# Where r and late q wait for their stores: pieces of the attention stage moved into the MLP's product buffer

## The chip, the cores and the metric

The kernel runs on one core of one Trainium2 chip. The metric is the device time of one execution in microseconds, the median of several. Before the change it is 825.69 us (median of five, 824.29 to 826.73).

## The reference, cut to what matters

The program computes a transformer block forward and all its gradients. A block is a pre-norm linear attention with a residual, then a pre-norm gated MLP with a residual; S = 2048 rows, D = 640, 32 heads of 20, F = 1728, bfloat16.

```python
phi = lambda t: jnp.where(t > 0, t + 1, jnp.exp(t)) + 1e-6
pq, pk = phi(q), phi(k)
kv  = einsum("bhsd,bhse->bhde", pk, v);  z = einsum("bhsd->bhd", pk)
o   = einsum("bhqd,bhde->bhqe", pq, kv) / (einsum("bhqd,bhd->bhq", pq, z)[..., None] + 1e-6)
h   = x + o_rows @ wo                       # x is layer-normed ahead of wqkv
h2  = h + (silu(hn @ w1) * (hn @ w3)) @ w2  # hn is layer-normed h
# outputs: h2, and the vjp of grad_out to x, wqkv, wo, w1, w3, w2
```

The names below: `pq` is phi(q); `r` is pq with each head divided by its denominator; `M` is the 640 x 640 product of pk and the normed x, from which kv comes; `hh` is the MLP's product silu(gate) * up.

## The kernel before

The rows are cut into 16 tiles of 128. Work is written out by hand in the order in which each engine runs it; no scheduler reorders it. Four instruction streams matter here beside TensorE: VectorE (DVE), ScalarE (ACT), GpSimd (POOL) and SyncE (SP). SP issues loads, stores and all DMA transposes (hardware queue q1); POOL issues stores (software queue q0). A DMA waits on its issuing engine for what it reads, so what is queued behind it on that engine waits too.

**First stage (to about 73 us).** k and q rows are projected and pass through phi; `m_part` and `m_end` build the blocks of M and copy them to `mbs` (4 blocks of 128 x 640); `dz` holds five diagonal 128 x 128 matrices for the denominators. `q_tile` and `q_home` put phi(q): tiles 0 to 3 and 8, 9 into `pq6` (6 tiles), tiles 4 to 7 into four rotating buffers `pql` of pool `pf`, tiles 10 to 13 into spare rows of `pkx`. `r_head`, `r_row` and `r_T` divide a tile in place and transpose it into `pqT` by a DMA transpose on SP.

**Transition (about 73 to 102 us), the tuple of steps in L834 to L842.** TensorE makes the last q tiles (`q_late`, L628) and the combined weight W' (`f2_wT`, L652): block i of W' is copied into `pkx` by ACT and DVE and transposed into `Wp` by a DMA transpose on SP (L660), five blocks, all behind `load_x(0, 4)` (640 KB, L185) on SP. Then `f2_half(t, j)` (L813, matmuls in L618) multiplies pqT by a half of Wp: half j = 0 reads blocks 0 to 2, half j = 1 blocks 2 to 4. The results are added to x, normed (`f2_hn`) and transposed on TensorE (`f2_ht`). In the same tuple POOL issues `r_store(4)`, `r4_out` (r of tiles 0 to 3, 640 KB from pq6, L683), `r_store(5)`, `f2_m_out`, `q_out(8, 10)` (320 KB from pq6, L680), `q_out(10, 14)` (640 KB from pkx) and `r_store(6)`; between the second and the third stands the product `r_prod(7)`, which waits for DVE.

**The MLP (about 102 to 345 us).** Four chunks c of 512 rows, each with 14 column blocks fc. Per block, TensorE makes gate and up (ten matmuls of 512) and one chunk of grad_out @ w2^T (`ghh`), ACT copies them out of PSUM, and per two blocks DVE runs seven products (`mlp_pair`, L768 to L786), of which POOL stores two (`gg_d`, 256 KB each) and SP one (`hh_d`). The four names sig, s2, gate, up rotate over two buffers of pool `pa`, so ACT's copy into `gate` (L749) of pair k waits until the `gg_d<-gate` store of pair k - 2 has landed. PSUM has four `mm` buffers. `hhT[c]`, the chunk's 14 x 512 products per partition (14,336 bytes), rotates over two buffers of `pa`; the next chunk multiplies it by w2. `r_steps` (L875) hangs the remaining q tiles on blocks of the MLP: `r_load(t)` (L689) reads phi(q) of tiles 8 to 15 back from DRAM (`pq_d`) into a `pql` buffer, `r_den` and `r_end` divide and store.

**Memory.** Pools are stacks at the left and right end of the SBUF. On the right lies `pf`, on it `p1` (among others pq6, mbs, dz, pkx), which is released at L843 and whose place `pa` takes; a tile of pa waits for every DMA and engine that still reads what lay there in p1.

**Later stages (345 us to the end)** make the gradients; they are not touched.

Of the kernel before, what the change touches and what calls it, by code (L numbers as in the profile page):

```python
# [9 lines left out]
P = 128  # L10
BF16 = mybir.dt.bfloat16
F32 = mybir.dt.float32
ALU = mybir.AluOpType
# [5 lines left out]
S, D, H, F = 2048, 640, 32, 1728  # L19
DH = D // H  # L20
ST, DT = S // P, D // P
FT, FP = 14, 1792
FL = F - 13 * P
W, SC, TPC = 512, 4, 4
# [31 lines left out]
def kernel(  # L56
# [19 lines left out]
    V, A, T, G, SY = nc.vector, nc.scalar, nc.tensor, nc.gpsimd, nc.sync  # L76
    dma, dmaT, dmaG = SY.dma_start, SY.dma_start_transpose, G.dma_start

    def rows(ap):
        return ap.rearrange("(t p) d -> p t d", p=P)  # L80
# [21 lines left out]
    r_v, pk_v, xn_v, hn_v, m_v, pq_v = rows(r_d), rows(pk_d), rows(xn_d), rows(hn_d), rows(m_d), rows(pq_d)  # L102

    def pool(name, side="left", space=None):
        kw = dict(space=space) if space is not None else dict(side=side)
        return tc.alloc_tile_pool(name=name, bufs=1, reuse_waits="tile", **kw)
# [10 lines left out]
    ident = cp.tile([P, P], BF16, name="ident")  # L117
    make_identity(nc, ident[:])
    ones = cp.tile([P, P], BF16, name="ones")
# [10 lines left out]
    class Stats:  # L130
# [8 lines left out]
        def run(self, src, a, b):  # L139
            for t in range(a, b):  # L140
                for j in range(2):
                    self.part(src, t, j)
# [30 lines left out]


    pf = pool("pf", "right")
    p1 = pool("p1", "right")
    ps = pool("p1p", space=PSUM)
    wqkv = U1.tile([P, DT, 3 * D], BF16, name="wqkv", tag="D")
# [56 lines left out]
    Z = cp.tile([P, DT], F32, name="Z")  # L235
# [14 lines left out]
    def p1_tr(t, parts=((0, DT),)):  # L250
        xn = x_sb[:, t, :]
        for a, b in parts:
            tr = ps.tile([P, DT, P], BF16, name="tr", bufs=2)
            for c in range(a, b):
                T.transpose(tr[:, c, :], xn[:, c * P:(c + 1) * P], ident[:])

            A.copy(out=pqT[:, a:b, t * P:(t + 1) * P], in_=tr[:, a:b, :])  # L257
# [13 lines left out]
    def p1_mm(t, n0, between=None):  # L271
        acc = p1_acc()
        for j in range(2):
            p1_half(acc[:, j, 0:HD], t, n0 + j * HD)
            if j == 0 and between is not None:
                between()
        return acc
# [20 lines left out]
            held.pop(0)()  # L298

    pqs = {}  # L300
    pq6 = p1.tile([P, 6, D], BF16, name="pq")

    def q_home(t):
        if t < 4 or 8 <= t < 10:
# [6 lines left out]
    pkx = []  # L311
# [5 lines left out]
    dz = {}  # L317

    def z_diag(m):
        dz[m] = p1.tile([P, P], BF16, name="dz", bufs=DT)  # L320
        V.tensor_scalar(out=dz[m][:], in0=ident[:], scalar1=Z[:, m:m + 1], scalar2=None, op0=ALU.mult)

    def z_late(ms, acc):

# [8 lines left out]
    def z_rows(parts, acc):  # L333

        for k, ms in enumerate(parts):
            for i, m in enumerate(ms):
                T.matmul(acc[:, k, i * P:(i + 1) * P], lhsT=ones[:], rhs=dz[m][:], start=(i == 0), stop=True,
                         skip_group_check=True)
        for k, ms in enumerate(parts):
            A.copy(out=Zb[:, ms[0] * P:(ms[-1] + 1) * P], in_=acc[:, k, 0:len(ms) * P])  # L340
# [60 lines left out]


    macc = {}
    mbs = p1.tile([P, 4, D], BF16, name="mbs")

    def m_part(m, tiles, js=(0, 1)):
        if m not in macc:
# [102 lines left out]
    for t in range(ST):  # L510
        k = p1_mm(t, D, (lambda: p1_tr(t + 1)) if t + 1 < XT_DMA else None)
# [96 lines left out]
    hn, hnT, hhT = {}, {}, {}  # L608
# [43 lines left out]
    def f2_wT(i):  # L652

        acc = [ps.tile([P, 512], F32, name="wt", tag=("o2", "at")[i % 2], bufs=2) for _ in range(2)]
        for c, a, b, bank, off, first in SQ:
            T.matmul(acc[bank][:, off:off + (b - a) * DH], lhsT=wo[:, c, i * P:(i + 1) * P],
                     rhs=bd[:, c, a * DH:b * DH], start=first, stop=True, skip_group_check=True)
        for bank, (a, b) in enumerate(((0, SPLIT_D), (SPLIT_D, H))):
            (A.copy, V.tensor_copy)[bank](out=pkx[0][:, i, a * DH:b * DH], in_=acc[bank][:, 0:(b - a) * DH])
        dmaT(out=Wp[:, :, i * P:(i + 1) * P], in_=pkx[0][:, i, :])  # L660
# [15 lines left out]
        dmaG(out=pq_v[:, 14:16, :], in_=qx[0][:, 0:4:2, :])  # L676

    def q_out(a, b):
        src = pq6[:, 4:6, :] if a == 8 else pkx[0][:, DT + a - 10:DT + b - 10, :]
        dmaG(out=pq_v[:, a:b, :], in_=src)  # L680

    def r4_out():
        dmaG(out=r_v[:, 0:4, :], in_=pq6[:, 0:4, :])  # L683

    def r_store(a, b):
        for t in range(a, b):
            dmaG(out=r_v[:, t, :], in_=pqs.pop(t))

    def r_load(t):  # L689
        pqs[t] = pf.tile([P, D], BF16, name="pql", bufs=4)[:]  # L690
        dma(out=pqs[t], in_=pq_v[:, t, :])

    def f2_hn(t):
        hn[t] = (pf.tile([P, D], BF16, name="hn", tag="pql", bufs=4) if t == 2 else
# [69 lines left out]
    def drain(n):  # L764
        for _ in range(min(n, len(later))):
            later.pop(0)()
# [63 lines left out]
    def kv3():  # L830
        for m in (2, 3, 4):
            f2_kv(m)

    run((q_late, 10, f2_mT), (q_late, 11, kv3), (phi_rest,), (r_store, 4, 5), (r4_out,),  # L834
        (q_late, 12, lambda: (f2_wT(0), f2_wT(1))), (q_late, 13, lambda: (f2_wT(2), f2_wT(3))),
        (phi_rest,), (q_late, 14, lambda: f2_wT(4)), (load_x, 4, 6), (r_head, 5), (r_prod, 7), (r_store, 5, 6),
        (f2_m_out,), (q_out, 8, 10), (q_out, 10, 14), (load_w2T, 8 * P, 10 * P), (mlp_ghh, 4), (q_late, 15), (sig_table,),
        (f2_half, 0, 0), (f2_half, 1, 0), (f2_half, 2, 0), (f2_half, 0, 1), (f2_half, 1, 1), (f2_hn, 0),
        (f2_half, 2, 1), (f2_hn, 1), (f2_half, 3, 0), (f2_hn, 2), (f2_half, 3, 1), (f2_ht, 0), (mlp_ghh, 5),
        (load_w2T, 10 * P, F), (f2_ht, 1), (mlp_ghh, 6), (r_red, 6, (0,)), (f2_hn, 3), (r_red, 6, (1,)), (f2_ht, 2),  # L840
# [3 lines left out]
    pa = pool("pa", "right")  # L844
# [26 lines left out]
    def r_end(t):  # L871
        r_scale(t)
        r_out(t)

    r_steps = [{2: ((r_load, 8),), 3: ((load_x, 6, 8),), 4: ((r_load, 9),), 5: ((r_store, 7, 8),),  # L875
                10: ((xn_out, 2, dmaG),), 12: ((r_load, 10),)},
               {0: ((r_den, 8), (load_x, 8, 12)), 1: ((r_end, 8), (r_load, 11), (xn_out, 3, dmaG)), 2: ((r_den, 9),), 3: ((r_end, 9), (r_load, 12)),
                4: ((r_den, 10), (q_rest,)), 5: ((r_end, 10), (r_load, 13)), 6: ((r_den, 11),),
# [1 line left out]
               {0: ((r_den, 13),), 1: ((r_end, 13),), 3: ((r_den, 14),), 4: ((r_end, 14),), 6: ((r_den, 15),),  # L880
                7: ((r_end, 15),), 10: ((w_out,),)}, {}]
    for c in range(SC):
        hhT[c] = pa.tile([P, FT, W], BF16, name="hhT", bufs=2)
        o2 = o2_steps(c - 1) if c > 0 else None

        def run_side(pos, fc):
            if c + 1 < SC:
                for f, i in sorted(sides[c][pos].get(fc, ()), key=lambda x: (x[0] is f2_ht, x[1])):
                    f((c + 1) * TPC + i)

        for fc in range(FT):
            mlp(c, fc, lambda: run_side(0, fc))
            drain(1)
            if o2 and not (c == SC - 1 and fc == 5):
                next(o2, None)
            run_side(1, fc)
            drain(1)
            if (c, fc) == (1, 5):
                load_x(12, 16)
            if c == 0 and fc in (5, 7, 9, 11):  # L900
                a, b = {5: (0, 3), 7: (3, 6), 9: (6, 10), 11: (10, 13)}[fc]
                dma(out=w2[:, a:b, :], in_=B_w2[a * P:b * P, :].rearrange("(c p) n -> p c n", p=P))
                if fc == 11:
                    dma(out=w2[0:FL, FT - 1, :], in_=B_w2[(FT - 1) * P:F, :])
            for f, *t in r_steps[c].get(fc, ()):
                f(*t)
            if c == 2 and fc == 3:
                dmaG(out=rows(kvT_d), in_=bd[:])
            if fc == (6, 3, 3)[min(c, 2)] and c < SC - 1:
                load_g2T(c + 1)  # L910
            if c == SC - 1 and fc == 0:
                g2 = U1.tile([P, ST, D], BF16, name="g2", tag="Q")
                tail = U2.tile([P, DT, P], BF16, name="w13tail", tag="g2T", bufs=2)
            if c == SC - 1 and fc in (1, 2, 5, 6):
                i = (1, 2, 5, 6).index(fc)
                dma(out=g2[:, i * TPC:(i + 1) * TPC, :], in_=goS[:, i * TPC:(i + 1) * TPC, :])
            if c == SC - 1 and fc == 8:
                dma(out=tail[:, :, 0:FL], in_=B_w1[:, F - FL:F].rearrange("(c p) f -> p c f", p=P))
                dma(out=tail[:, :, FL:P], in_=B_w3[:, 0:P - FL].rearrange("(c p) f -> p c f", p=P))
            if c == SC - 1 and fc == 9:  # L920
                wT2 = U1.tile([P, DT, D], BF16, name="wT2", tag="MW")
                dmaT(out=wT2[:], in_=w_d[:, :])
# [14 lines left out]
    for _ in o2_steps(SC - 1, A.dma_start, "at"):  # L937
        drain(1)
    pa.release()
    pf.release()  # L940
    ps.release()

# [38 lines left out]
    for fc in range(FT - 1):  # L981
        b, i = divmod(fc, 4)
        if fc == FT - 2:
            gw2_tail()
        acc = ps.tile([P, 2, 512], F32, name="gw", bufs=4)
        for j in range(2):
            for t in range(ST):
                T.matmul(acc[:, j, 0:HD], lhsT=hb[b][:, t, i * P:(i + 1) * P], rhs=g2[:, t, j * HD:(j + 1) * HD],  # L988
                         start=(t == 0), stop=(t == ST - 1))
# [155 lines left out]
    for t in range(ST):  # L1145
# [14 lines left out]
        if t >= 1:  # L1160
# [3 lines left out]
            if t <= 2 * DT:  # L1164
                n = (t - 1) % DT
                dst, src = (woT, A_wo) if t <= DT else (kvN, kvT_d)
# [23 lines left out]
    a, b = ST - 1, ST - 2  # L1190
# [90 lines left out]
    for m, (a, b) in enumerate(M_H):  # L1281
        n = (b - a) * DH
        acc = ps.tile([P, 512], F32, name="gkvT", tag="dkv", bufs=3)
        for c in range(DT):
            T.matmul(acc[:, 0:n], lhsT=woT[:, c, m * P:(m + 1) * P], rhs=QT[:, c, a * DH:b * DH], start=(c == 0),
                     stop=(c == DT - 1))
# [38 lines left out]
    acc = d_acc()  # L1325
    for m in range(DT):
        T.matmul(acc[:, m // 4, m % 4 * P:(m % 4 + 1) * P], lhsT=ones[:], rhs=gzd[:, m, :], start=(m % 4 == 0),
                 stop=True, skip_group_check=True)
# [3 lines left out]
    for t in range(ST):  # L1332
        c, i = divmod(t, TPC)
        u = t // 2
        acc = d_acc()
        for j in range(2):
            for k in range(DT):
                T.matmul(acc[:, j, 0:HD], lhsT=xnT[c][:, k, i * P:(i + 1) * P], rhs=gm[:, k, j * HD:(j + 1) * HD],  # L1338
                         start=(k == 0), stop=(k == DT - 1))
# [7 lines left out]
        if t in (2, 5, 8, 11, 14):  # L1347
            n = t // 3
            acc = square(mN, gkv_b, n)
            k = (4, 0, 1, 2, 3)[n]  # L1350
# [7 lines left out]
        if t in (6, 8, 10, 12):  # L1358
            n = t // 2 - 3
# [110 lines left out]
```

## Time and profile before

| | |
|---|---|
| median of five runs | 825.69 us |
| the profiled execution's own time | 827.82 us |
| its span in the trace | 826.1 us |
| TensorE clock granted | 1.00 |
| busy: TensorE, DVE, ACT, POOL | 815.9, 452.9, 323.7, 133.1 us |
| bytes by queue: q1 (SP), q0 (POOL), q10 (ACT) | 115.54, 24.81, 16.34 MB |
| HBM read and written | 47.33 and 51.46 MB |

How to read it: an idle time is put down to what ended it ("1.94 <-DMA Wp<-pkx": idle 1.94 us, until a DMA into Wp landed). In a group of merged rows the time is from the first start to the last end. The row of a DMA on SPq or POOLq is the time in which its engine issues it, not that of the transfer; the time to landing is listed apart. The share of a DMA queue is the time of its packets over all 16 DMA engines; it can pass 100% because packets overlap. Matmuls are pipelined: five of 128 x 512 in a row start 1.08 us after the five before them when nothing holds them.

### The profile page before, as it was taken

What the parts mean: (1) busy time and instruction counts of PE and PEld (TensorE: products, weight loads), DVE (VectorE), ACT (ScalarE), POOL (GpSimd) and SP (SyncE); (2) the same over time, 40 slices, a digit from 0 to 9 for tenths busy, and PEclk for the clock granted to TensorE, in tenths of its full rate; (3) what the DMA queues carried; (4) which work ended last, traced back from release to release, by engine and by line L of the source; (5) the groups of instructions that cost most, each with busy time, mean ns of one, the idle gap of its engine ahead of it and who ended that gap; (6) DMA issues with size and microseconds to landing.
All of it is one profiled execution on the core that took longest, in us unless ns stands there. A gap on an engine that the chain in (4) does not pass through costs nothing.

```text
span 826.1 us, 14203 instructions
## 1 busy us (share of the span) xinstructions
PE 815.9 (99%) x5549; PEld 523.0 (63%) x5549; DVE 452.9 (55%) x961; ACT 323.7 (39%) x607; POOL 133.1 (16%) x194
## 2 busy tenths in 40 slices
PE   8999899999999999999999999999999999999998
PEld 6777544555555555777777777777777777555554
DVE  7869788899898666400057777772681545200000
ACT  7856577765655666011121221222212334211111
POOL 2244333233323212100001111110220000000000
PEclk9999999999999999999999999999999999999999
DMA  9999979796575565999777787359984798985771
GB/s 226 263 277 238 232 184 269 239 217 175 136 210 158 152 209 161 228 239 271 222 163 181 188 217 180 85 101 184 274 206 96 163 191 181 210 195 136 167 167 38
DMA packets 320947, 157.59 MB, mean 191 GB/s; under 512 B 238704, under 2 KB 314064, under 8 KB 320880
## 3 DMA queue, kind: packets, MB, share of 16 engines
q1 hardware_dynamic: 278768, 115.54, 61.7%
q0 software_dynamic: 7392, 24.81, 8.8%
q10 hardware_dynamic: 34720, 16.34, 8.7%
q8 instruction: 43, 0.70, 0.4%
q14 instruction: 24, 0.20, 0.1%
HBM read 47.33 MB, written 51.46 MB: 120 GB/s over the span
## 4 chain that ended last, share of the span: by engine, by line
PE 85%; DVE 9%; DMA 3%; ACT 1%; issue 1%; POOL 0%; ACTq 0%; DVEq 0%; POOLq 0%
PE job L1234 19%; PE ghn L1033 14%; PE mm L380 11%; PE gxn L1392 8%; PE gw L988 7%; PE o L799 6%; PE big L265 4%; PE gwo L1118 3%; PE macc L411 3%; PE gr L1090 3%; PE dkv L1338 3%; DMA gg_d<-gate 2%; DVE s L774 2%; DVE gate L774 1%; DVE st L147 1%
## 5 line engine op out<-in xcount | busy, mean ns | idle before, releaser
L1234 PE MATMUL job<-gb,hnN 128*128 128x432 bf16 (+2 forms) x656 | 117.0, 342 | 0.0
L1033 PEld LDWEIGHTS <-ggb 128*128 128x128 bf16 x864 | 84.5, 98 | 32.8
L1234 PEld LDWEIGHTS <-hnN 128*128 128x128 bf16 x656 | 63.6, 98 | 53.4
L380 PE MATMUL mm<-pqT,w 128*128 128x512 bf16 x405 | 93.6, 379 | 0.1
L380 PEld LDWEIGHTS <-w 128*128 128x128 bf16 x540 | 52.5, 98 | 63.1 <-issue 1.1
L1238 ACT CAST obs<-job 128x432 bf16<-128x432 f32 (+3 forms) x61 | 29.3, 481 | 123.0 <-PE job L1234 123.0
L799 PE MATMUL o<-w,hhT 128*128 128x320 bf16 x448 | 67.7, 299 | 0.0
L1033 PE MATMUL ghn<-w13a,ggb 128*128 128x320 bf16 x448 | 63.5, 299 | 0.0
L1033 PE MATMUL ghn<-w13b,ggb 128*128 128x320 bf16 x416 | 61.4, 299 | 0.0
L380 PE MATMUL mm<-g2T,w2T 128*128 128x512 bf16 x240 | 59.6, 379 | 0.0
L799 PEld LDWEIGHTS <-hhT 128*128 128x128 bf16 x448 | 43.8, 98 | 23.8 <-issue 0.2
L988 PE MATMUL gw<-g,hb 128*128 128x320 bf16 x416 | 56.8, 299 | 0.0
L1098 POOL TENSOR_TENSOR sz<-Zb,g_h 128x640 f32<-128x640 bf16 x16 | 20.2, 1261 | 198.8 <-DVE g_h L1096 198.8
L988 PEld LDWEIGHTS <-hb 128*128 128x128 bf16 x416 | 40.6, 98 | 16.0 <-issue 0.3
L1392 PE MATMUL gxn<-wqT,gT 128*128 128x320 bf16 x320 | 48.7, 299 | 0.0
L400 ACT CAST ghh<-mm 128x512 bf16<-128x512 f32 x48 | 28.5, 594 | 39.3 <-PE mm L380 34.5
L738 ACT ACTIVATE sig<-mm 128x512 bf16<-128x512 f32 x56 | 33.9, 605 | 24.1 <-PE mm L380 20.1
L1045 ACT ACTIVATE gs<-ghn 128x640 bf16<-128x640 f32 x16 | 11.3, 704 | 78.7 <-PE ghn L1033 78.7
L265 PE MATMUL big<-wqkv,pqT 128*128 128x320 bf16 x260 | 39.9, 299 | 1.5 <-DMA wqkv<-in_A_wqkv_dram 0.9
L380 PEld LDWEIGHTS <-w2T 128*128 128x128 bf16 x260 | 25.3, 98 | 23.3
L265 PEld LDWEIGHTS <-pqT 128*128 128x128 bf16 x320 | 30.6, 98 | 14.3 <-ACT pqT L257 1.2
L1392 PEld LDWEIGHTS <-gT 128*128 128x128 bf16 x320 | 31.3, 98 | 12.2
(208 smaller groups left out, 1280.7 us busy)
## 6 DMA issues: line engine op xcount, KB each, us to landing
hh_d<-hhT SPq DMA_DIRECT2D x24, 256.0 KB, 2.6
gg_d<-gate POOLq DMA_DIRECT2D x24, 256.0 KB, 4.9
gg_d<-ghh POOLq DMA_DIRECT2D x24, 256.0 KB, 3.6
ggb<-gg_d SPq DMA_DIRECT2D x6, 896.0 KB, 5.3
ggb<-gg_d ACTq DMA_DIRECT2D x6, 832.0 KB, 5.9
out_dram<-obs ACTq DMA_DIRECT2D x39, 108.0 KB, 3.1
x_sb<-in_A_x_dram SPq DMA_DIRECT2D x6, 640.0 KB, 5.9
ggb<-gg_d SPq DMA_DIRECT2D x2, 1728.0 KB, 13.5
```

Source lines behind the costliest of these rows:

```text
L265: T.matmul(acc, lhsT=pqT[:, c, t * P:(t + 1) * P], rhs=wqkv[:, c, n0:n0 + HD], start=(c == 0), stop=(c == DT - 1))
L380: T.matmul(acc[:], lhsT=w[:, c, fc * P:(fc + 1) * P], rhs=rhs[:, c, :], start=(c == 0), stop=(c == DT - 1))
L400: A.copy(out=ghh[n // 2][:, n % 2, :], in_=acc[:])
L411: T.matmul(macc[m][j][:, 0:n], lhsT=pk_all[:, t, m * P:(m + 1) * P], rhs=x_ext[:, t, j * HD:j * HD + n], start=(t == 0), stop=(t == ST - 1))
L738: A.activation(sig[:, i, :], gp[:], AF.Sigmoid)
L774: V.tensor_tensor(out=out, in0=a, in1=b, op=alu)
L799: T.matmul(o2["ps"][:, 0:HD], lhsT=hhT[c][:, fc, i * P:(i + 1) * P], rhs=w2[:, fc, j * HD:(j + 1) * HD], start=(fc == 0), stop=(fc == FT - 1))
L988: T.matmul(acc[:, j, 0:HD], lhsT=hb[b][:, t, i * P:(i + 1) * P], rhs=g2[:, t, j * HD:(j + 1) * HD], start=(t == 0), stop=(t == ST - 1))
L1033: T.matmul(acc[:, j, 0:HD], lhsT=ggb[t // 2][:, k, lo:lo + P], rhs=rhs[:, j * HD:(j + 1) * HD], start=(k == 0), stop=(k == NG - 1))
L1234: T.matmul(acc[:, 0:n], lhsT=lhs[:, t, m * P:(m + 1) * P], rhs=rhs(t), start=(t == 0), stop=(t == ST - 1))
L1238: A.copy(out=ob, in_=acc[:, 0:n])
L1392: T.matmul(acc[:, j, 0:HD], lhsT=g, rhs=wqT[:, k, j * HD:(j + 1) * HD], start=(k == 0), stop=(k == 14))
```

## The change

A new pool `ph` lies between `pf` and `p1`, with one buffer of 14,336 bytes per partition. In the first stage it holds `hx`: the six tiles of pq6, the four blocks of mbs and the five dz matrices (11 x 640 numbers per partition), which leave p1. In the MLP the same buffer is hhT of the chunks 1 and 3; hhT of chunks 0 and 2 has one buffer in `pa`. So the six q tiles stay in place through chunk 0.

Four things follow in the order of the work: `r4_out` goes out of the transition and is issued as two stores of 320 KB, at blocks 1 and 4 of chunk 0; `q_out(8, 10)` is gone, and `r_load(8)` and `r_load(9)` read the tiles from `hx` by a copy inside the SBUF; `r_store(4)` is joined with `r_store(5)`, behind `r_prod(7)` on POOL; pool addresses of p1 and pa shift, and with them the waits of pa's first tiles.

```diff
+    ph = pool("ph", "right")
...
-    pq6 = p1.tile([P, 6, D], BF16, name="pq")
+    hx = ph.tile([P, FT * W], BF16, name="hx", tag="H1")[:, 0:11 * D].rearrange("p (t n) -> p t n", n=D)
+    pq6, mbs = hx[:, 0:6, :], hx[:, 6:10, :]
...
-        dz[m] = p1.tile([P, P], BF16, name="dz", bufs=DT)
+        dz[m] = hx[:, 10, m * P:(m + 1) * P]
...
-    mbs = p1.tile([P, 4, D], BF16, name="mbs")
...
     def q_out(a, b):
-        src = pq6[:, 4:6, :] if a == 8 else pkx[0][:, DT + a - 10:DT + b - 10, :]
-        dmaG(out=pq_v[:, a:b, :], in_=src)
-
-    def r4_out():
-        dmaG(out=r_v[:, 0:4, :], in_=pq6[:, 0:4, :])
+        dmaG(out=pq_v[:, a:b, :], in_=pkx[0][:, DT + a - 10:DT + b - 10, :])
+
+    def r4_out(a, b):
+        dmaG(out=r_v[:, a:b, :], in_=pq6[:, a:b, :])
...
     def r_load(t):
+        src = pqs[t] if t < 10 else pq_v[:, t, :]
         pqs[t] = pf.tile([P, D], BF16, name="pql", bufs=4)[:]
-        dma(out=pqs[t], in_=pq_v[:, t, :])
+        dma(out=pqs[t], in_=src)
...
-    run((q_late, 10, f2_mT), (q_late, 11, kv3), (phi_rest,), (r_store, 4, 5), (r4_out,),
+    run((q_late, 10, f2_mT), (q_late, 11, kv3), (phi_rest,),
         (q_late, 12, lambda: (f2_wT(0), f2_wT(1))), (q_late, 13, lambda: (f2_wT(2), f2_wT(3))),
-        (phi_rest,), (q_late, 14, lambda: f2_wT(4)), (load_x, 4, 6), (r_head, 5), (r_prod, 7), (r_store, 5, 6),
-        (f2_m_out,), (q_out, 8, 10), (q_out, 10, 14), (load_w2T, 8 * P, 10 * P), (mlp_ghh, 4), (q_late, 15), (sig_table,),
+        (phi_rest,), (q_late, 14, lambda: f2_wT(4)), (load_x, 4, 6), (r_head, 5), (r_prod, 7), (r_store, 4, 6),
+        (f2_m_out,), (q_out, 10, 14), (load_w2T, 8 * P, 10 * P), (mlp_ghh, 4), (q_late, 15), (sig_table,),
...
-    r_steps = [{2: ((r_load, 8),), 3: ((load_x, 6, 8),), 4: ((r_load, 9),), 5: ((r_store, 7, 8),),
+    r_steps = [{1: ((r4_out, 0, 2),), 2: ((r_load, 8),), 3: ((load_x, 6, 8),), 4: ((r_load, 9), (r4_out, 2, 4)),
+                5: ((r_store, 7, 8),),
...
-        hhT[c] = pa.tile([P, FT, W], BF16, name="hhT", bufs=2)
+        hhT[c] = (ph.tile([P, FT, W], BF16, name="hhT", tag="H1") if c % 2 else
+                  pa.tile([P, FT, W], BF16, name="hhT"))
...
     pa.release()
+    ph.release()
     pf.release()
```

More of the change, by code (lines that the diff above doesn't have):

```diff
@@ L319, in z_diag @@
     def z_diag(m):
-        dz[m] = p1.tile([P, P], BF16, name="dz", bufs=DT)
-        V.tensor_scalar(out=dz[m][:], in0=ident[:], scalar1=Z[:, m:m + 1], scalar2=None, op0=ALU.mult)
+        dz[m] = hx[:, 10, m * P:(m + 1) * P]
+        V.tensor_scalar(out=dz[m], in0=ident[:], scalar1=Z[:, m:m + 1], scalar2=None, op0=ALU.mult)
     def z_late(ms, acc):
@@ L336, in z_rows @@
             for i, m in enumerate(ms):
-                T.matmul(acc[:, k, i * P:(i + 1) * P], lhsT=ones[:], rhs=dz[m][:], start=(i == 0), stop=True,
+                T.matmul(acc[:, k, i * P:(i + 1) * P], lhsT=ones[:], rhs=dz[m], start=(i == 0), stop=True,
                          skip_group_check=True)
```

## The prediction, made before the result was known

> **What bounds the kernel now.** I read the page first, then TensorE's waits, then the timeline around the longest of them, then the DMA queues in that stretch, and last the MLP's first chunk, where work is put in.
>
> The page, and TensorE's waits (microseconds in total, times, longest):
>
> ```profile
> PE 815.9 (99%) x5549; PEld 523.0 (63%) x5549; DVE 452.9 (55%) x961; ACT 323.7 (39%) x607; POOL 133.1 (16%) x194
> ```
>
> ```profile
> PE at L618 <- DMA Wp<-pkx: 3.7, 2, 1.9
> PE warm L450 <- DVE zero L124: 1.1, 1, 1.1
> ...
> PE at L618 <- DVE rden L359: 0.3, 1, 0.3
> ```
>
> TensorE is idle for 826.1 - 815.9 = 10.2 us of the span. Most of that is the start and the tail; the one wait inside that is worth anything is 3.7 us for the transposes into Wp, in the transition, where the change takes stores away. The timeline of it (start, length, engine):
>
> ```profile
> 76.07 0.60 POOL L687 DMA_DIRECT2D r_d<-pql  x1 [0.98 <-DVE mq L292]
> ...
> 76.67 0.76 POOL L683 DMA_DIRECT2D r_d<-pq  x1
> 76.70 2.94 SPq L370 DMA_TRANSPOSE pqT<-pql  x1
> ...
> 80.62 8.02 SPq L660 DMA_TRANSPOSE Wp<-pkx  x5
> ...
> 87.88 2.20 PE L618 MATMUL at<-Wp,pqT 128*128 128x320 bf16 x15 [1.94 <-DMA Wp<-pkx]
> ...
> 91.94 0.85 PE L618 MATMUL at<-Wp,pqT 128*128 128x320 bf16 x5 [1.73 <-DMA Wp<-pkx]
> ```
>
> TensorE stops at 85.94, waits 1.94 for the third block of Wp, runs three halves, waits 1.73 for the fifth. The reader is to see the second and third row: POOL issues 640 KB of r just as SP issues the transpose ahead of Wp's, and that issue lasts 2.94 us where its like lasts 1.2 (the one at 75.38 lasts 1.22). The DMA queues from 78.9 to 80.5 (packets, MB, share of 16 engines), and the third and fifth transposes into Wp in narrow windows of SP's timeline:
>
> ```profile
> q0 software_dynamic: 143, 0.65, 101.2%
> q1 hardware_dynamic: 16, 0.00, 0.6%
> ```
>
> ```profile
> 83.37 1.99 SPq L660 DMA_TRANSPOSE Wp<-pkx  x1
> ...
> 87.19 1.45 SPq L660 DMA_TRANSPOSE Wp<-pkx  x1
> ```
>
> For 1.6 us the 16 DMA engines move POOL's stores alone; SP's queue stands. It then has to move a transpose, 640 KB of x and the five transposes in turn.
>
> The first chunk of the MLP:
>
> ```profile
> 117.09 0.74 POOL L757 DMA_DIRECT2D gg_d<-gate  x1 [1.68 <-ACT s L739]
> 118.90 0.72 POOL L757 DMA_DIRECT2D gg_d<-ghh  x1 [1.06 <-DVE ghh L774]
> ```
>
> ```profile
> 130.15 2.32 PE L380 MATMUL mm<-pqT,w 128*128 128x512 bf16 x10
> ```
>
> ```profile
> 130.74 0.59 ACT L749 CAST gate<-mm 128x512 bf16<-128x512 f32 x1 [2.46 <-DMA gg_d<-gate]
> ```
>
> ACT's copy into gate waits for a store to land, four times here, 7.1 us between 110 and 147; TensorE does not stand, but barely. The ten matmuls at 130.15 take 2.32 us, their plain time, and the second five (due at 130.15 + 1.08 = 131.23) need the PSUM buffer that this copy frees at 130.74 + 0.59 = 131.33. There is no slack left.
>
> **The change, part by part.** Times are those of the profiled execution: span 826.1, own time 827.82, which is 2.1 over the median of the runs (825.69). I make the sum against 827.82 and carry the difference to the median.
>
> *1. r4_out, and r_store(4), leave the stretch 76 to 81.* That is 640 + 160 KB, the two POOL rows at 76.07 and 76.67. The worth is read from the chain to the fifth block of Wp:
> - First block: its source in pkx is complete when DVE's two casts at 79.67 (0.76) are half through, about 80.1. SP issued it at 80.62, because of the 2.94 us. At 1.2 the issue would be free by 78.0, the load of x (0.71) by 78.8. So the first goes out at about 80.1, 0.5 earlier.
> - Each next one costs 1.2 and a gap of 0.1. The third, then, is issued at 82.7 (was 83.37) and the fifth at 85.3 (was 87.19): the third's 1.99 and a gap of 0.5 before the fifth come from a queue that is behind, and go with it. The sources are there in time (the last DVE cast ends at 83.9).
> - Landing: the fourth took 2.9 us, the fifth 4.7, with POOL's stores of 86.89 to 88.72 beside it. Those start no earlier than now, except r_store(4), and the fifth is now ahead of most of them. I take 3.6: it lands at 88.9, was 91.9.
> - The third, with 3.6 to 4.5, lands at 86.3 to 87.2; three halves of 0.69 end at 88.4 to 89.3. So TensorE takes up the second halves at about 88.9 instead of 91.94: **3.0 us earlier**. No more than 3.67 can come of it. The low end is 0.5, if only the first block's issue moves.
>
> Does it carry on? From 91.94 to 147 TensorE never idles for more than 0.3 us, and DVE's norms (idle until 93.29 for the second halves) follow it; DMAs needed there (x of tiles 4 and 5, issued 88.71, used at 101.58) have over 6 us. So the whole rest moves forward.
>
> *2. r_store(4) behind r_prod(7) on POOL.* It is issued at about 85.9, after r_prod(7) (84.38 + 1.53), and not at 76.07. Nothing on POOL waits longer: the stores behind it waited for DVE until 86.89. Its landing frees the pql buffer that the norm of tile 2 writes at 97.44 (94.4 when 3.0 earlier); the stores' times to landing here are 2.1 to 4.7, so 90.6 at the latest. Cost 0; without that cover it would hold DVE.
>
> *3. q_out(8, 10) goes* (POOL, 0.72 at 88.02, 320 KB). It lay beside the fifth block's landing, counted above. q_out(10, 14) goes out 0.7 earlier for it.
>
> *4. r_load(8) and (9) read the SBUF.* Same two DMAs on SP, 0.44 and 0.53 to issue, at 111.72 and 117.97. The copy within the SBUF has no row; the loads from DRAM landed in 3.7 to 6.9 us, a store from SBUF in 2.1. The tiles are used at 152.01, over 27 us later: 0 at either end.
>
> *5. r4_out in the MLP.* Two POOL issues of about 0.72, 320 KB (0.33 MB) each. On the page q0 moved 24.81 MB in 8.8% of the span, 2.93 us for a MB, so 0.96 us of all DMA engines for each.
> - The first stands behind r_store(6) and a memset (end 105.77) and waits for nothing; POOL's next store is at 111.09, after 5.3 us idle. From 104 to 110 the queues are 7.6% and 15.7% busy: 0.
> - The second stands between the gate store at 117.09 and the ghh store at 118.90; POOL's 1.06 idle there covers its issue. But its data go ahead of ghh, r_store(7) and the third gate store, whose landing (130.7) TensorE has no slack for, and from 117 to 131 the queues are 75.4% and 34.1% busy. Bounds: 0 and, for all 640 KB, 1.92; I take **0.7**, most of one store.
>
> *6. The places.* The tiles of p1 and pa lie elsewhere. In the program, the first sigmoid and the first s product no longer wait for stores of the transition; the last of these, from pkx, landed at 88.72 + 6.3 = 95.0, before 102.80, so 0. The first hhT product of chunk 1 now waits for the second r4_out and r_load(9): about 125 against 148: 0. Matmuls, DVE and ACT work are the same; POOL issues one DMA less.
>
> Sum: 827.82 - 3.0 + 0.7 = 825.5, and from the median 825.69 - 2.3 = **823.4 us**. About 0.2% (1.65 us) is what a measurement of this kernel can tell from no change; 2.3 is 0.28%.
>
> **Two rules beside these rows.** The Trainium skill, "DMA: Bandwidth & Descriptors", section "SWDGE vs HWDGE vs iDMA", says that a DMA engine takes its software and hardware queues in turn. The rows of 78.9 to 80.5 show no such sharing; by the rule the stores would have held SP's queue for half as long, and the sum would lose about 1 us of gain (824.4). The row decides. The same page, "Queues, rings and completion order", speaks against the change: a completion is written only after every earlier write of that DMA engine, on whatever queue. The gate store of 121.81 landed 8.9 us later, close to the transpose of grad_out issued at 120.95 (10.2 us), which fits it. By the rule alone the second r4_out would hold that landing for its whole 0.96, and the sum would be 823.7.
>
> **The rivals.**
> - *No gain: SP's transposes are late by themselves.* Idle DMA engines are seen at 77.5 to 78.4, before any of POOL's bytes move, while SP is in its 2.94; one elsewhere is long without POOL's stores (2.11 at 53.68). Then only the 0.5 of the first issue goes, 0.5 - 0.7 = +0.2: 825.9. Against it: the 0.6% row, and the transpose at 229.34, 2.89 long just after POOL issued 256 and 800 KB.
> - *Slower: r4_out holds the gate stores.* Place: ACT's L749 in chunk 0. If the second gate store (5.3 us to landing, 117.09 to 122.36) lands as late as the third (8.9), TensorE, with 0.2 slack there (copy free at 122.95, needed at 123.12), stands 3.4, and a further 0.96 at the third: 4.4 - 3.0 = +1.4, 827.1. It decides as soon as the stalls there exceed 3.0 us. For it: four waits without slack. Against it: the first half falls into idle queues, and the second is behind that gate store, not ahead.
> - *Full gain: both waits for Wp go and the MLP hides all*: 825.69 - 3.7 = 822.0.
>
> **How the numbers follow.** Forecast (net -1.7 to -3.0) 0.50, full gain (beyond -3.0) 0.13, no gain 0.21, slower rival 0.16. Faster by over 0.2%: 0.13 + 0.47 + 0.02 from the others = 0.62. The slower rival's middle is within 0.2%, but its stalls may recur at later pairs: 0.12 slower, 0.04 within; same 0.03 + 0.19 + 0.04 = 0.26. The range goes from full gain, 821.9, over no gain, to 826.2, leaving about 0.05 below and 0.14 above. The forecast's own range is 822.7 to 824.0.
>
> **What the profile after would show.** The issue of r4's transpose near 1.2 us; Wp's five transposes within 6.5 us from 80.1; TensorE's wait for Wp at 0.7 and not 3.7; the MLP's first matmuls near 98.4 (101.52 now). Chunk 0's gate copies waiting 2 to 3.4 us, with one stall of TensorE under 1. I am wrong if the wait for Wp stays above 2, or if TensorE stands for over 2 us between 110 and 150.

## The result, and the profile after

| | median, us | executions (lowest to highest) |
|---|---|---|
| before | 825.30 | 79 (823.74 to 832.38) |
| after | 824.35 | 44 (823.64 to 826.37) |
| profiled execution, before | 827.82 (span 826.1) | |
| profiled execution, after | 825.21 (span 823.5) | |

The ratio is 0.9984, with a 95% interval of 0.9978 to 0.9991. The kernel is faster by 1.0 us by the medians and by 1.3 us by the ratio, where 2.3 us were forecast. That is about half of the forecast gain. It is inside the stated range (821.9 to 826.2) but outside the forecast's own 822.7 to 824.0, and the 0.16% of the ratio are less than the 0.2% that the prediction thought would more likely than not be passed. Two things in the table matter for what follows. The fastest executions of the two kernels are alike (823.74 and 823.64). And the execution that was profiled before lies 2.5 us above the median of the 79.

TensorE's wait for Wp after (total, times, longest), and the timeline of the transition (start, length, engine):

```profile
PE at L619 <- DMA Wp<-pkx: 1.3, 1, 1.3
```

```profile
77.03 2.20 SPq L372 DMA_TRANSPOSE pqT<-pql  x1
...
79.32 0.53 SPq L186 DMA_DIRECT2D x_sb<-in_A_x_dram  x1
...
81.22 7.04 SPq L661 DMA_TRANSPOSE Wp<-pkx  x5
...
86.83 2.20 PE L619 MATMUL at<-Wp,pqT 128*128 128x320 bf16 x15
86.91 0.60 POOL L687 DMA_DIRECT2D r_d<-pql  x1
...
90.51 0.85 PE L619 MATMUL at<-Wp,pqT 128*128 128x320 bf16 x5 [1.34 <-DMA Wp<-pkx]
```

The wait for the third block is gone and that for the fifth is 1.34 instead of 1.73, so 3.7 us have become 1.3. The transpose of r of tile 4 still takes 2.20 us to issue although no store of POOL is beside it. The row at 86.91 is r_store(4) in its new place.

The first chunk of the MLP: TensorE's matmuls, and ACT's waits for the gate stores between 90 and 150 us.

```profile
100.08 8.80 PE L382 MATMUL mm<-pqT,w 128*128 128x512 bf16 x40
```

```profile
ACT gate L750 <- DMA gg_d<-gate: 3.3, 3, 2.4
```

These waits were 7.1 us and are 3.3, with 640 KB of r added between them. TensorE has no wait here.

To see where time goes, I matched each group of matmuls in the trace of before with the same group in the other trace and took the difference of their starts. For after it is +1.06 us at 70 us (before the transition), -1.43 at 110 us, -2.15 at 230 us, and -2.62 at the end. So the start of this execution lost 1.06; the transition gained 2.49; the MLP gained 0.72 and the tail 0.46. The loss at the start is TensorE waiting for its first loads; it was 0.30 and 0.38 in two further profiles of the same kernel, and 1.21 in one of the kernel before, so it comes and goes.

### The profile page after: what moved, and what is told of

Its sections match the earlier page's. It is cut to its first block, busy times and chain, and to the rows that moved or that the text cites. A ratio compares the mean times of both kernels' runs of the same rounds, so it can differ in the third digit from the quotient of the medians.

```text
span 823.5 us, 14204 instructions
## 1 busy us (share of the span) xinstructions
PE 816.3 (99%) x5549; PEld 523.6 (64%) x5549; DVE 453.3 (55%) x961; ACT 324.5 (39%) x607; POOL 132.6 (16%) x194
## 4 chain that ended last, share of the span: by engine, by line
PE 97%; DMA 1%; SPq 1%; ACT 0%; issue 0%
PE mm L382 20%; PE job L1238 19%; PE ghn L1037 14%; PE gxn L1396 8%; PE o L800 7%; PE gw L992 7%; PE big L266 4%; PE gwo L1122 3%; PE macc L412 3%; PE gr L1094 3%; PE dkv L1342 3%; PE at L619 2%; PE mm L266 1%; DMA g2T<-in_grad_out_dram 1%; PE dkv L1270 1%; PE gp L382 1%
```

## The experiments

Three accounts of the missing half had to be told apart. One: r4_out holds SP's queue in the transition, as forecast, but the profiled execution of before had an unusually long wait for Wp, so that its 3.7 us were not there to be gained in the median. Two: the gain in the transition is the same in every execution, and the MLP takes half of it back through the moved stores of r. Three: the gain has another source (the q tiles that stay in the chip, the new places in memory), and r4_out is not what makes Wp late.

### The two kernels again

> The kernel before, profiled once more: it tells which differences between the two profiles are the kernel's. Theory (the 1.06 us by which the changed kernel's profile is late from the start, 9 to 18 us, is chance): start-up differs from the first profile by up to 1 us, the two waits for Wp are 3.7 +- 0.5 us again. Rival (the new places make the start slower): start-up agrees with the first profile within 0.2 us.

> The changed kernel once more, with times. Theory: 0.997 to 0.999 of before; wait for Wp 1.3 us, once; start-up anywhere between the first profile of before and 1.06 us later; no stall of TensorE in chunk 0 of the MLP. Rival (new places slow the start): start-up late by 1.06 us again. Rival (the second r4_out costs in most executions): TensorE stands 0.5 to 1 us between 115 and 135.

> The kernel before once more, for another profile of its own. Theory (the profiled execution of 827.82 had an extraordinary share of its excess in the wait for Wp): this execution, whatever its time T, waits about 2.2 + (T - 825.5) / 2 us for Wp, so 2 to 3 us when T lies between 825 and 827, and the stalls of 0.2 to 0.3 at about 145 and 195 us are there. Rival (the wait is the same in every execution and the excess lay elsewhere): 3.5 to 3.9 us whatever T is.

> The kernel after once more, beside the two that follow. 824.2 to 824.7; the wait for Wp 1.0 to 1.7 us in one piece; the five transposes within 6.9 to 7.1 us, with the gap of some 0.4 before the fifth.

The kernel after took 824.51 us (825.44 for before on that chip; ratio 0.9988, 0.9980 to 0.9997) and 824.45 us (825.41; 0.9981, 0.9967 to 0.9995). The table has the profile of each of these executions, and of three kernels that follow. "Third" is SP's time to issue Wp's third transpose; "five" is the whole row of five; "fifth lands" is from the issue of the fifth to its landing.

| profile | its own time | r of tile 4: issue | third | five | fifth lands | wait for Wp |
|---|---|---|---|---|---|---|
| before | 827.82 | 2.94 | 1.99 | 8.02 | 4.7 | 3.7 |
| before, second | 826.64 | 2.85 | 1.54 | 7.34 | 3.7 | 2.7 |
| before, third | 826.29 | 2.14 | 1.82 | 7.52 | 3.4 | 1.7 |
| r4_early | 826.08 | 2.89 | 2.09 | 7.81 | 4.2 | 2.8 |
| after | 825.21 | 2.20 | 1.20 | 7.04 | 3.6 | 1.3 |
| after, second | 824.78 | 2.19 | 1.20 | 6.88 | 3.9 | 1.7 |
| after, third | 824.46 | 1.63 | 1.21 | 6.88 | 3.2 | 1.0 |
| before_rT4 | 824.09 | behind | 1.22 | 6.50 | 2.6 | 0 |
| rT4_again | 823.58 | behind | 1.22 | 6.50 | 3.3 | 0.7 |

The waits of the third execution of before, for the row that the verdict rests on:

```profile
PE at L618 <- DMA Wp<-pkx: 1.7, 2, 1.2
```

The wait for Wp in the kernel before is 3.7, 2.7 and 1.7 us in three executions; in the kernel after it is 1.3, 1.7 and 1.0. The forecast rested on the longest one, and the second account falls with it. (The 3.7 us expected of the second execution of before and the 2.6 us expected of the third were too many.) That execution also lacks two short stalls of TensorE, 0.23 us at 145 us and 0.49 us at 195 us, which were expected in it, which the first profile of before has, and which the first profile of after has not. So those 0.72 us in the MLP come and go, and the kernel before can be without them. Whether the change makes them rarer is not shown: a loss of 0.4 to 0.5 us at 195 us is in three of the four profiles with the old memory layout (before three times, and before_rT4, below), and in one of the ten with the new (rT4_late; both_late has some 0.2 us of it).

### r4_out back in the transition

```diff
-    run((q_late, 10, f2_mT), (q_late, 11, kv3), (phi_rest,),
+    run((q_late, 10, f2_mT), (q_late, 11, kv3), (phi_rest,), (r4_out, 0, 4),
...
-    r_steps = [{1: ((r4_out, 0, 2),), 2: ((r_load, 8),), 3: ((load_x, 6, 8),), 4: ((r_load, 9), (r4_out, 2, 4)),
+    r_steps = [{2: ((r_load, 8),), 3: ((load_x, 6, 8),), 4: ((r_load, 9),),
```

> The changed kernel with the store of r of tiles 0 to 3 (640 KB, one DMA) put back to its old place in the transition; q tiles 8 and 9 still stay in the SBUF, r_store(4) stays late. Theory (this store holds SP's transposes): the transition is slower again by 2 to 2.5 us, two waits for Wp of 3 to 3.7 us, time 1.000 of before or up to 1.001. Rival (the places or the 320 KB of q tiles make the gain): the wait for Wp stays 1.3 us and the time stays at 0.998.

Measured: 825.18 us against 824.51 for the kernel after on that chip; the ratio to before is 0.9993 (0.9982 to 1.0003). The waits and the transition of this kernel:

```profile
PE at L619 <- DMA Wp<-pkx: 2.8, 2, 1.5
```

```profile
75.01 0.81 POOL L683 DMA_DIRECT2D r_d<-hx  x1
...
76.01 2.89 SPq L372 DMA_TRANSPOSE pqT<-pql  x1
...
78.99 0.54 SPq L186 DMA_DIRECT2D x_sb<-in_A_x_dram  x1
...
80.13 7.81 SPq L661 DMA_TRANSPOSE Wp<-pkx  x5
```

With r4_out alone put back (r_store(4) stays late), both waits for Wp return (2.8 us, short of the 3 to 3.7 expected), and so do the third's 2.09 us and the row of 7.81. So r4_out does make Wp late in this order of SP's queue. (It goes out at 75.01, earlier than in the kernel before, since r_store(4) is no longer ahead of it.) How much of it the median holds is another matter: this profiled execution took 826.08 us, 0.9 over the median of its kernel and the longest but one, which took 4076.28. By the medians r4_out costs 0.67 us, and part of that is not the wait: the tail, after the last matmuls, is 0.38 us longer than in the kernel after. So some 0.3 us are left for the wait.

### Both stores of r into the block that has no slack

```diff
-    r_steps = [{1: ((r4_out, 0, 2),), 2: ((r_load, 8),), 3: ((load_x, 6, 8),), 4: ((r_load, 9), (r4_out, 2, 4)),
+    r_steps = [{2: ((r_load, 8),), 3: ((load_x, 6, 8),), 4: ((r_load, 9), (r4_out, 0, 2), (r4_out, 2, 4)),
```

> The changed kernel with both halves of r4_out at block 4 of chunk 0, so 640 KB and not 320 go in between the second gate store and the ghh store. It doubles the suspected cost in the MLP. If the 0.7 us of the prediction were there: TensorE stands 1.5 to 2 us in chunk 0, time 0.999 to 1.001. If the store is hidden as the first profile shows: not over 0.3 us slower than the changed kernel, 0.998.

Measured: 824.44 us against 824.51, ratio to before 0.9990 (0.9981 to 0.9999). ACT's waits for the gate stores in this kernel:

```profile
ACT gate L750 <- DMA gg_d<-gate: 2.9, 3, 1.9
```

Doubling the bytes at block 4 neither costs time that these runs can tell nor lengthens the waits. The MLP takes nothing back, and the rival that it does falls.

### Phi(q) of tiles 8 and 9 through DRAM again

```diff
-        dmaG(out=pq_v[:, a:b, :], in_=pkx[0][:, DT + a - 10:DT + b - 10, :])
+        src = pq6[:, 4:6, :] if a == 8 else pkx[0][:, DT + a - 10:DT + b - 10, :]
+        dmaG(out=pq_v[:, a:b, :], in_=src)
...
-        src = pqs[t] if t < 10 else pq_v[:, t, :]
+        src = pq_v[:, t, :]
...
-        (f2_m_out,), (q_out, 10, 14), (load_w2T, 8 * P, 10 * P), (mlp_ghh, 4), (q_late, 15), (sig_table,),
+        (f2_m_out,), (q_out, 8, 10), (q_out, 10, 14), (load_w2T, 8 * P, 10 * P), (mlp_ghh, 4), (q_late, 15), (sig_table,),
```

> The kernel after, but phi(q) of tiles 8 and 9 goes to DRAM in the transition as before (320 KB from POOL, between the store of M and the store of tiles 10 to 13) and is loaded back from there. Theory (the gain is r4_out's and the layout's; those 320 KB are issued after the fifth Wp transpose): the wait for Wp grows by at most 0.5 us over the 1.0 to 1.7 of the kernel after, time 824.4 to 824.9; no stall over 0.1 at about 145 and 195 us. Rival (tiles 8 and 9 staying in the chip are what removes these two stalls): 0.5 to 0.6 us come back there, time 824.9 to 825.4.

Measured: 824.40 us (825.37 for before on that chip; ratio 0.9986, 0.9975 to 0.9997), wait for Wp 1.0 us, and neither of the two short stalls. The kernel after took 824.51 and 824.45 us on the two other chips, and 824.35 in the table at the top. This part of the change is worth nothing that these runs can tell.

### r of tile 4 transposed behind Wp

After the experiments above, 1.0 to 1.7 us of wait are left in the kernel after. Its five transposes begin when the casts let them, but the row is 6.9 to 7.0 us long, since about 0.5 us passes before the fifth, and the fifth takes 3.2 to 3.9 us to land where the three before it take 2.6 to 2.8. Two moves ask what holds it.

```diff
-    r_head(4)
+    r_row(4)
...
-        (phi_rest,), (q_late, 14, lambda: f2_wT(4)), (load_x, 4, 6), (r_head, 5), (r_prod, 7), (r_store, 4, 6),
+        (phi_rest,), (q_late, 14, lambda: f2_wT(4)), (r_T, 4), (load_x, 4, 6), (r_head, 5), (r_prod, 7), (r_store, 4, 6),
```

> The kernel after, but the transpose of r of tile 4 (SP, 2.20 us to issue, the last but one ahead of Wp's first) goes behind Wp's five. Theory (Wp's first is held by the casts into pkx, and the five then follow at 1.3 us each): the first is issued at the same time as in the kernel after, Wp waits 1.0 to 1.7 us, time 824.2 to 824.7. Rival (SP's queue is still behind from that transpose and the load of x): Wp's transposes are issued in 1.2 each without the gap before the fifth, the wait falls under 0.6 us, time 823.2 to 823.8.

> The kernel after with the transpose of r of tile 4 behind Wp's five, once more. If its 823.64 is its own: 0.5 to 1.0 under the kernel after on this chip, 823.4 to 823.9, the five transposes within 6.5 us. If it was the chip's or chance: within 0.3 of the kernel after.

Measured: 823.64 us beside 824.40 for q8_early and 825.37 for before on the same chip (ratio 0.9975, 0.9963 to 0.9987); and 823.59 beside 824.45 for the kernel after and 825.41 for before on another (0.9979, 0.9962 to 0.9997). The five transposes take 6.50 us in both and the wait for Wp is 0.6 and 0.7 us. The first goes out no earlier, as the theory said, but the gap ahead of the fifth is gone and the time falls, as the rival said. The edit is worth 0.8 to 0.9 us on top of the change (on the first chip q8_early stands in for the kernel after).

The traces say more about that gap. SP's rows around it, in after and then in rT4_again:

```profile
85.17 1.20 SPq L661 DMA_TRANSPOSE Wp<-pkx  x1
...
86.88 1.37 SPq L661 DMA_TRANSPOSE Wp<-pkx  x1
```

```profile
86.79 1.32 SPq L372 DMA_TRANSPOSE pqT<-pql  x1
88.56 0.45 SPq L186 DMA_DIRECT2D x_sb<-in_A_x_dram  x1
```

The pause has not gone. It stands two DMAs later, behind all five transposes of Wp, where it costs TensorE nothing. Count the instructions of SP that a trace records (its DMAs and its waits for semaphores): in all 14 profiles a pause of 0.43 to 0.45 us stands ahead of the 80th. That is Wp's fifth transpose where r of tile 4 is ahead of Wp, and the load of x where it is behind. Ahead of the 208th, 336th and 464th, 128 apart each time, SP pauses too, for 0.34 to 0.38 us wherever it does not wait for something else there. So this pause goes with the place in SP's program and not with what its queue holds, and part of what the edit gains is that Wp's fifth transpose comes ahead of that place. Why SP pauses there is not shown by any run.

The second move takes POOL's stores of M and of phi(q) of tiles 10 to 13 away from the fifth block's landing, alone (q10_late) and with the first move (both_late).

```diff
-        (f2_m_out,), (q_out, 10, 14), (load_w2T, 8 * P, 10 * P), (mlp_ghh, 4), (q_late, 15), (sig_table,),
+        (load_w2T, 8 * P, 10 * P), (mlp_ghh, 4), (q_late, 15), (sig_table,),
...
-        (r_inv, 6), (r_scale, 6), (r_T, 6), (mlp_ghh, 7), (f2_ht, 3), (f2_half, 4, 0), (f2_half, 4, 1), (r_red, 7), (r_inv, 7),
+        (r_inv, 6), (r_scale, 6), (r_T, 6), (mlp_ghh, 7), (f2_ht, 3), (f2_half, 4, 0), (f2_half, 4, 1), (f2_m_out,), (q_out, 10, 14), (r_red, 7), (r_inv, 7),
```

> As rT4_late, and the stores of M and of phi(q) of tiles 10 to 13 (640 KB from POOL, issued at 87.4 to 89.8 in the kernel after, beside the landing of the fifth Wp block) go behind, to just before the last reduction of the transition. Theory (the fifth block's landing of 3.6 us is its own, and TensorE's 1.0 to 1.7 us come from the casts and five transposes in a row): time as rT4_late within 0.3. Rival (these stores stretch that landing): it falls from 3.6 to about 2.9 as the fourth's, the wait by 0.7, time 0.7 under rT4_late.

> The kernel after with the stores of M and of phi(q) of tiles 10 to 13 (POOL, 640 KB and M's last block) behind, just before the transition's last reduction; r of tile 4 is transposed where the kernel after does it. If this place of the stores is what cost the kernel with both moves 0.8 over the one with the transpose alone: 0.5 to 1.0 over the kernel after, 824.9 to 825.4, with a new or longer wait in the first blocks of the MLP or at 95 to 105 us. If these stores stretched the fifth block's landing: 0.3 to 0.7 under it. If neither: within 0.3.

Measured: both_late 824.43 us (825.37; 0.9987, 0.9975 to 0.9999), q10_late 824.75 us (825.41; 0.9984, 0.9969 to 0.9999). The fifth block lands in 3.3 us in both and the wait is 0.7 and 1.1 us, so these stores were not what stretched that landing. Nor does the time agree with either expectation of both_late. The later place costs 0.8 us with the first move, by the medians, and 0.3 us alone, which is within the spread of the executions (824.10 to 825.10, beside 823.92 to 825.21 for the kernel after). Both profiles show one thing that the other twelve do not: DVE's first product into hhT, which lies where pkx lay, waits 0.7 us for the moved store of phi(q) (at 106.17 in q10_late), and at 117 us TensorE loses 0.17 (q10_late) and 0.24 us (both_late). That the one leads to the other was not tried, and the rest of the 0.8 us stays open.

### The same transpose, in the kernel before

If the order on SP is what matters, the layout and the moved stores are not needed. This kernel is the one before, with all its stores of the transition where they were, and only the transpose of r of tile 4 behind Wp's:

```diff
-    r_head(4)
+    r_row(4)
...
-            dmaG(out=r_v[:, t, :], in_=pqs.pop(t))
+            dmaG(out=r_v[:, t, :], in_=pqs[t])
...
-        (phi_rest,), (q_late, 14, lambda: f2_wT(4)), (load_x, 4, 6), (r_head, 5), (r_prod, 7), (r_store, 5, 6),
+        (phi_rest,), (q_late, 14, lambda: f2_wT(4)), (r_T, 4), (load_x, 4, 6), (r_head, 5), (r_prod, 7), (r_store, 5, 6),
```

> The kernel before with one thing moved: the transpose of r of tile 4 on SP goes behind Wp's five, while r_store(4), r4_out and both pieces of phi(q) stay in the transition. Theory A (the 640 KB of r4_out hold whatever SP has in its queue then, now the load of x and Wp's first transposes): the wait for Wp stays at 1.7 to 3.7 us, time 825.0 to 825.8, and the executions keep their spread (825.4 plus or minus 1.2). Theory B (the long issue of that one transpose, 2.1 to 2.9 us, is what the stores stretch, and Wp's are late only as they are queued behind it): the first of Wp goes out at 80.15 and the five take 6.5 us, wait 0.6 to 0.9, time 823.7 to 824.3.

Measured: 823.82 us (823.26 to 824.64) beside 825.41 for before and 824.45 for after on the same chip. That is 1.6 us under before by the medians; the ratio, 0.9964 (0.9945 to 0.9982), says 3.0 us, as it counts the long executions of before on that chip (up to 832.19). All that TensorE waits for in this kernel, and its transition:

```profile
PE warm L450 <- DVE zero L124: 1.1, 1, 1.1
PE big L265 <- ACT pqT L257: 0.4, 1, 0.4
PE big L265 <- DMA wqkv<-in_A_wqkv_dram: 0.3, 1, 0.3
PE at L618 <- DVE rden L359: 0.3, 1, 0.3
```

```profile
76.16 0.60 POOL L687 DMA_DIRECT2D r_d<-pql  x1 [0.98 <-DVE mq L292]
...
76.53 1.49 SPq L185 DMA_DIRECT2D x_sb<-in_A_x_dram  x1
...
76.76 0.76 POOL L683 DMA_DIRECT2D r_d<-pq  x1
...
80.25 6.50 SPq L660 DMA_TRANSPOSE Wp<-pkx  x5
...
88.20 0.85 PE L618 MATMUL at<-Wp,pqT 128*128 128x320 bf16 x5
```

There is no wait for Wp at all. The 800 KB of r go out at 76.16 and 76.76 as before, and the queues show them just as dense; from 78.98 to 80.58 (packets, MB, share of 16 engines):

```profile
q0 software_dynamic: 112, 0.55, 96.0%
q1 hardware_dynamic: 4, 0.01, 0.9%
```

So the stores still stop SP's queue for 1.6 us, but that no longer matters with one transpose less in it ahead of Wp's. Theory A falls; theory B holds in the time and in the 6.50 us of the five, while its 0.6 to 0.9 us of wait were too many. With the transpose of r of tile 4 ahead of Wp's, the wait is 1.0 to 1.7 us without r4_out on POOL (the kernel after) and 2.8 with it (r4_early). With the transpose behind, it is 0.6 and 0.7 us without r4_out (rT4_late, rT4_again) and 0 with it (this kernel). Each of these kernels but the kernel after has one or two profiles. By them r4_out makes Wp late only where that transpose is ahead; the transpose costs something without r4_out too, and moving it gains more. That is the first account, with a second condition that the forecast had not seen. What these runs do not part is how much of the transpose's cost is its own time in the queue, and how much is SP's pause, which by being there it puts ahead of Wp's fifth.

## Why the prediction was half right

**The sum's base: the step that failed.** "I make the sum against 827.82 and carry the difference to the median" took a wait of 3.7 us, which belongs to that execution, into the median. With the wait gone (before_rT4, whose profile is shorter than that of before by 3.82 us in the transition and by nothing that counts elsewhere) the median falls by 1.6 us. So about 1.6 us is what the median execution of before had to give. The kernel after still has 1.0 to 1.7 us of wait, and a tail 0.46 us shorter; its gain of 1.0 us, by estimate, is then about 0.5 us from the transition and the other half from the tail, which no step of the sum had. The 2.1 us by which the profiled execution stood over the median was not spread over it: much of it lay in the very wait that the change shortens. That the result came inside the range was in part luck: the range was 4.3 us wide, and the tail's share was not foreseen.

**Step 1, r4_out leaves the transition.** Against the same execution the size was nearly right: 3.0 us forecast, 2.49 measured, and 2.16 and 2.83 in the other two profiles of after. The first block goes out at 80.16 (81.22 less the 1.06 of the start), as forecast; it does so in the third profile of before too. The MLP's first matmuls start at 99.0 on that clock (100.08 less 1.06), not 98.4, as 1.3 us of wait stayed and not 0.7. Two details of the step were wrong. The issue of r of tile 4's transpose did not fall to 1.2 us: it is 1.6 to 2.2 without any store beside it, which costs nothing as the casts decide. And the gap before the fifth block did not "come from a queue that is behind": it is there in all ten profiles with that transpose ahead of Wp's, and two DMAs later in the four with it behind, always ahead of SP's 80th recorded instruction. This is the 0.5 us by which the step fell short: the fifth was issued at 85.8 on the clock of before (86.88 less 1.06) and not at 85.3, and in this profile it landed 3.6 us later, as forecast.

**Step 2, r_store(4) later, at 0.** Not 0: its new place, at 85.8 on the clock of before, is beside the landing of the fifth block. In before_rT4, where it goes out at 76.16, the fifth lands in 2.6 us; in rT4_again, with the same six DMAs of SP in the same order, it lands in 3.3 us. The queues in the stretch from 86.6 to 88.1, rT4_again first, then before_rT4:

```profile
q1 hardware_dynamic: 654, 0.16, 58.4%
q0 software_dynamic: 36, 0.16, 32.7%
```

```profile
q1 hardware_dynamic: 682, 0.17, 58.2%
```

The 0.16 MB of q0 are r_store(4), and they go with 0.7 us of wait. This reading compares two kernels that differ in more than this store; it was not tried alone.

**Steps 3 and 4, q_out(8, 10) and the loads from the SBUF, at 0.** Right: q8_early undoes both within 0.1 us.

**Step 5, r4_out in the MLP, at 0.7.** It costs nothing that the runs can tell, even doubled. The forecast looked at how full the queues were and how little slack the third gate store had, and took the new bytes as delay for that store. It landed earlier, in 5.7 us and not 8.9, so the 0.96 us that the prediction's second rule would have added to that landing do not show either; the last section shows what moved.

**Step 6, the places, at 0.** Nothing in the profiles contradicts that; the tail's 0.46 us is not theirs, as r4_early has the new places and not that gain.

**The rivals.** "Slower" fell: the gate copies wait 3.3 us in all, as the forecast's own case had it, and TensorE not at all. "Full gain" did not come, since 1.3 us of wait stay. "No gain" had its reason wrong, as the stores do make Wp late, but it had noted that a transpose of SP can be slow to issue without them, and so it is.

**The skill's rule.** The Trainium skill, "DMA: Bandwidth & Descriptors", section "SWDGE vs HWDGE vs iDMA", has the two kinds of queue take turns on a DMA engine. Two rows say different things on it. In before_rT4 above, q0 has 96.0% and q1 0.9% for 1.6 us, in 112 and 4 packets, which does not look like taking turns. In r4_early, from 78.88 to 80.48, both move:

```profile
q1 hardware_dynamic: 536, 0.14, 71.4%
q0 software_dynamic: 67, 0.26, 41.0%
```

So the runs do not settle how the queues share.

## What to carry to other kernels

Where a forecast takes most of its gain from one wait in one profiled execution, and that execution lies well over the median, price the wait by what the median can contain: here the profile had 3.7 us and the median some 1.6. A wait for a DMA has a queue in front of it on two sides, the other queue's bytes and its own queue's earlier entries; look first for an entry of the same queue that nobody needs yet, since moving one such transpose (823.82 us) did more than moving 800 KB of stores and rearranging the memory (824.45 us). The two together took 823.59 us, the lowest median of this study, though executions of 823.53 us and up are not told apart from the 823.26 to 824.64 of the transpose alone. r_store(4) put back early in that kernel is the next thing to try and was not run. And where an engine pauses with nothing to wait for, count its instructions before you blame its queue: here two such pauses, SP's in the transition and POOL's in the tail, stood at one place of the program in every profile, and adding or moving an instruction ahead of them changed what they held up.

## What was not expected

**A delay that pulled a store forward.** The third gate store of chunk 0 landed 8.8 to 9.2 us after its issue in the three profiles of before, in before_rT4 and in r4_early, and in 5.6 to 8.0 us in the nine kernels and repeats that store r in the MLP. What changes is the order against SP's transpose of grad_out (SP's timeline and the store's time to landing, before and then after):

```profile
120.95 5.51 SPq L223 DMA_TRANSPOSE g2T<-in_grad_out_dram  x1
```

```profile
gg_d<-gate POOLq DMA_DIRECT2D x1, 256.0 KB, 8.9
```

```profile
119.97 6.29 SPq L224 DMA_TRANSPOSE g2T<-in_grad_out_dram  x1
```

```profile
gg_d<-gate POOLq DMA_DIRECT2D x1, 256.0 KB, 5.7
```

In before the transpose goes out 0.86 us ahead of the gate store (121.81), in after 0.39 us ahead (120.36). Beside the second r4_out, SP's load of w just ahead takes 0.97 us to issue instead of 0.51, and so the transpose starts later against the store. Over the 14 profiles, 0.85 or 0.86 us ahead goes with 8.8 to 9.2 us to land, and 0.60 us or less with at most 8.0 (5.6 to 5.9 where it is 0.39 or less and only the second half of r4_out stands there). That the order is the cause was not tried.

**A tail shorter by 0.45 us.** The last store of the program, by ACT, is issued at 823.11 in before and at 820.95 in after:

```profile
823.11 0.34 ACTq L1239 DMA_DIRECT2D out_dram<-obs  x1
```

```profile
820.95 0.34 ACTq L1243 DMA_DIRECT2D out_dram<-obs  x1
```

From there to the end of the span (826.1 and 823.5) it is 2.99 and 2.55 us. All nine profiles with r's stores in the MLP have the shorter tail; the four of the kernel before and its variant, and r4_early, have the longer one. The traces show a pause of POOL behind it. POOL's recorded instructions number 329 in the four profiles of the longest tail, 330 in r4_early, and 331 or 332 in the nine. In the first five, POOL pauses 0.35 or 0.36 us ahead of its 325th, which belongs to the closing steps that the end of the span waits for. In the nine, the 325th comes earlier in the closing steps or ahead of them, where POOL waits some 200 us for the other engines in any case, and no such pause is left behind the last store. So the shorter tail goes with how many instructions POOL has, and not with where r is stored; no run changed that number alone. It is about half of what this change gained in the median.
